# Loading the second FFN weight in chunks of 6, 5, 2 and 1 blocks of 128 rows

## Chip, cores, metric

One core of one Trainium2 chip at a time. The metric is the device time of one execution in microseconds (us). "Span" is the time from first to last instruction in a profiled execution, some 1.8 us shorter than the device time.

In the lines of the profile PE is TensorE doing matmuls, PEld its weight loads, DVE is VectorE, and SPq the queue that issues the large loads. L448 is a line of the kernel. u_ps is the result of the first FFN matmul, z_ps that of the second. A load (DMA) is cut into packets and shared out over 16 DMA engines; each of them adds 1 to the load's semaphore, a counter that other engines wait for, when its share is done. A load has landed with the 16th increment.

## The reference, cut to what matters

A decode step for 4 tokens of width 512: adaptive layer norm, attention over the last 1024 cached keys and values, then a small FFN with a gate.

```python
x = x + ga * _A_ref(h, A_k_cache, A_v_cache, A_wq, A_wo)
h = _layernorm(x, axis=-1) * (1 + cb) + sb
x = x + gb * _B_ref(h, B_w1, B_w2)      # relu(h @ w1) @ w2, w1 512x1792, w2 1792x512, bf16
```

The inputs are 32 MB, the arithmetic is small. w2's 1792 rows are 14 blocks of 128.

## The kernel before

All large loads go through one queue, in this order: keys, w_mod, wq, more keys, values, wo, w1, w2. w1 and w2 stand last; the FFN is what remains when they have landed.

```python
nc.sync.dma_start(out=w1_sb, in_=B_w1.rearrange("(p t) n -> p t n", t=DT))
E4 = 4
...
for m4 in range(FT4):                       # three chunks of 4 blocks, 512 KB each
    nc.sync.dma_start(out=w2_dst[:, m4 * E4 * D:(m4 + 1) * E4 * D], in_=w2_src[:, m4, :])
nc.sync.dma_start(...)                      # the last 2 blocks, 256 KB
...
def w1_cols(t, m):                          # a chunk of e blocks gives partition q its rows q*e .. q*e+e-1,
    f0, e = ...                             # so block m takes every e-th column of w1
    return w1_sb[:, t, f0 + m % E4:f0 + e * P:e]

def ffn1(m0, m1):     # 4 matmuls for each block, then three DVE operations for the group -> uT32
    ...
def ffn2(m0, m1):     # 4 matmuls for each block, side by side in four column groups, summed in z_ps
    ...
for (m0, m1) in [(0, 2 * E4), (2 * E4, FT)]:
    ffn1(m0, m1)
for (m0, m1) in U_GROUPS:                   # blocks 0-3, 4-7, 8-11, 12-13
    ffn2(m0, m1)
zg = z_ps * gb2 ; res = zg + x12_ps         # two DVE operations (written out in the kernel)
nc.sync.dma_start(out=out..., in_=res[::BS, :])
```

The first matmul that reads a chunk waits for the chunk's semaphore, so the chunk sizes set where PE waits.

Of the kernel before, what the change touches and what calls it, by code (L numbers as in the profile page):

```python
# [17 lines left out]
def kernel(  # L18
# [14 lines left out]
    nc = tc.nc  # L33
    P = 128
    B, Sq, D = A_x.shape
    _, Hkv, S, Dh = A_k_cache.shape
# [3 lines left out]
    Dff = B_w1.shape[1]  # L40
    DT = D // P
    FT = Dff // P
# [57 lines left out]
    for h in range(Hkv):  # L100
        vt_ = kvpool.tile([P, NI, Dh], bf16, tag="kv", name=f"v{h}")
        nc.sync.dma_start(
            out=vt_[:].rearrange("p j d -> p (j d)"),
            in_=A_v_cache[:, h, S - W:, :].rearrange("b (p j) d -> p b (j d)", j=NI),
# [13 lines left out]
    w1_sb = w12[:, 0:DT * Dff].rearrange("p (t n) -> p t n", t=DT)  # L118
    w2_sb = w12[:, DT * Dff:DT * Dff + FT * D].rearrange("p (m n) -> p m n", m=FT)
    nc.sync.dma_start(out=w1_sb, in_=B_w1.rearrange("(p t) n -> p t n", t=DT))  # L120

    E4 = 4
    FT4 = FT // E4
    F4 = FT4 * E4 * P
    w2_dst = w12[:, DT * Dff:DT * Dff + FT * D]
    w2_src = B_w2[0:F4, :].rearrange("(m q e) n -> q m (e n)", q=P, e=E4)
    for m4 in range(FT4):
        nc.sync.dma_start(out=w2_dst[:, m4 * E4 * D:(m4 + 1) * E4 * D], in_=w2_src[:, m4, :])
    nc.sync.dma_start(out=w2_dst[:, FT4 * E4 * D:FT * D], in_=B_w2[F4:Dff, :].rearrange("(q e) n -> q (e n)", q=P))
    U_GROUPS = [(m, min(m + E4, FT)) for m in range(0, FT, E4)]  # L130


    nc.scalar.preload_act_table_set("natural_log_exp_and_others")
# [87 lines left out]
    m4 = const.tile([P, B], f32, name="m4")  # L221
# [67 lines left out]
    for par in range(2):  # L289
        dst = qpad_s[:, :, par * NHW * CG:(par + 1) * NHW * CG].rearrange("p b (h c) -> p b h c", h=NHW)  # L290
        nc.vector.tensor_copy(  # L291
            out=dst[:, :, :, 16 * par:16 * par + rep],
            in_=qT_ps[:, par].rearrange("p h r b -> p b h r"))
# [35 lines left out]
    for iq in range(NQ):  # L329
        ws = slice(iq * WQ, (iq + 1) * WQ)  # L330
        nc.scalar.activation(out=e_sb[:, ws].rearrange("q (u k e) -> q u k e", k=KC, e=2),  # L331
                             in_=sc_ps[:, ws].rearrange("q (u e k) -> q u k e", e=2, k=KC), func=ACT.Exp,
# [92 lines left out]
    nc.scalar.activation(out=rstd2[:], in_=mm[:], func=ACT.Exp, scale=-0.5)  # L425

    def w1_cols(t, m):
        f0, e = (m // E4 * E4 * P, E4) if m < FT4 * E4 else (F4, 2)
        return w1_sb[:, t, f0 + m % E4:f0 + e * P:e]

    z_ps = psA.tile([NH * CG, DH2], f32, tag="t", name="z_ps")

    def ffn1(m0, m1):
        u_ps = psA.tile([P, m1 - m0, 2, B], f32, tag="t", name=f"u_ps_{m0}")
        for m in range(m0, m1):
            for t in range(DT):
                nc.tensor.matmul(out=u_ps[:, m - m0].rearrange("p s b -> p (s b)"), lhsT=w1_cols(t, m),  # L437
                                 rhs=ab[:, t].rearrange("p s b -> p (s b)"), start=(t == 0), stop=(t == DT - 1))
        us = work.tile([P, m1 - m0, B], f32, name=f"us_{m0}")
        nc.vector.tensor_tensor(out=us[:], in0=u_ps[:, :, 0, :], in1=rstd2[:].unsqueeze(1).to_broadcast([P, m1 - m0, B]),  # L440
                                op=ALU.mult)
        nc.vector.tensor_tensor(out=us[:], in0=us[:], in1=u_ps[:, :, 1, :], op=ALU.add)
        nc.vector.tensor_scalar_max(out=uT32[:, m0:m1, ::BS], in0=us[:], scalar1=0.0)

    def ffn2(m0, m1):
        for m in range(m0, m1):
            for nh in range(NH):
                nc.tensor.matmul(out=z_ps[nh * CG:(nh + 1) * CG, :], lhsT=uT32[:, m, :],  # L448
                                 rhs=w2_sb[:, m, nh * DH2:(nh + 1) * DH2],
                                 start=(m == 0), stop=(m == FT - 1), tile_position=(0, nh * CG))  # L450

    for (m0, m1) in [(0, 2 * E4), (2 * E4, FT)]:
        ffn1(m0, m1)
    for (m0, m1) in U_GROUPS:
        ffn2(m0, m1)

    zg = work.tile([NH * CG, DH2], f32, name="zg")
    nc.vector.tensor_tensor(out=zg[:], in0=z_ps[:], in1=gb2[:], op=ALU.mult)  # L458
# [33 lines left out]
```

## Time and profile before

| | before |
|---|---|
| device time, median (range) | 86.10 us (86.03 to 86.45), 3 runs; 86.19 with three more, made beside the changed kernel |
| span of the profiled run | 84.4 us |
| DMA engines busy | 90% or more from 2 to 78 us, in all slices but one |
| PE busy | 65%, off the chain of waits except at the end |

The chain and the tail's timeline are shown in the prediction. One more pair of lines: a group of the page (busy us, mean ns; then idle us ahead of it and what ended it), and the page's count of DMA packets.

```profile
L437 PE MATMUL u_ps<-ab,w 128*128 128x8 bf16 x56 | 2.0, 174 | 1.0 <-DMA w<-in_B_w_dram 1.0
DMA packets 4606, 32.14 MB, mean 381 GB/s; under 512 B 493, under 2 KB 501, under 8 KB 2037
```

### The profile page before, as it was taken

The numbers are of one execution on the slowest core, as the hardware profiler recorded it, in microseconds if no ns is written. First come the engines' busy times: TensorE is split into PE (matmuls) and PEld (weight loads), VectorE is DVE, ScalarE is ACT, GpSimd is POOL, SyncE is SP. The second block draws the span as 40 slices with busy tenths as digits, with TensorE's granted clock in tenths as the row PEclk, the third lists the DMA queues.
The fourth block names the chain that finished last, engine by engine and source line by source line (L and its number), as shares of the span: only waits on it lengthen the run. The fifth ranks groups of instructions, "written<-read, shape, count | busy, mean of one in ns | idle before, by whom it ended". The sixth has DMA issues, their size and how long they took to land.

```text
span 84.4 us, 2416 instructions
## 1 busy us (share of the span) xinstructions
PE 55.3 (65%) x1092; PEld 46.9 (56%) x1092; DVE 24.8 (29%) x70; ACT 23.1 (27%) x36; POOL 4.4 (5%) x18
## 2 busy tenths in 40 slices
PE   0029980496351899999998079994645379678640
PEld 0029970594351739788774079984542059568520
DVE  0033443013300104845546694500011020241320
ACT  2314471001200007977776376010000010020000
POOL 6940000000000000000000000000000000000000
PEclk9999999555555559999999965975555555555555
DMA  0999998999999999999999999999999999999500
GB/s 2 316 415 450 501 419 384 450 411 435 419 408 423 404 427 423 431 408 415 423 419 419 423 415 423 423 415 419 402 404 406 410 424 436 418 385 407 211 0 2
DMA packets 4606, 32.14 MB, mean 381 GB/s; under 512 B 493, under 2 KB 501, under 8 KB 2037
## 3 DMA queue, kind: packets, MB, share of 16 engines
q1 hardware_dynamic: 4580, 31.99, 91.9%
q8 instruction: 8, 0.13, 0.6%
q10 hardware_dynamic: 16, 0.01, 0.0%
q14 instruction: 2, 0.01, 0.0%
HBM read 31.99 MB, written 0.00 MB: 379 GB/s over the span
## 4 chain that ended last, share of the span: by engine, by line
DMA 92%; SPq 2%; PE 1%; DVE 1%; issue 0%
DMA v<-in_A_v_cache_dram 26%; DMA wo_sb<-in_A_wo_dram 24%; DMA wq_sb<-in_A_wq_dram 23%; DMA w<-in_B_w_dram 19%; SPq L82 1%; PE z_ps L448 1%; SPq L91 1%; DVE zg L458 0%; DVE res L460 0%
## 5 line engine op out<-in xcount | busy, mean ns | idle before, releaser
L203 ACT COPY kT<-ktp 128x1024 bf16<-128x1024 bf16 x16 | 15.5, 1017 | 15.9 <-PE ktp L198 14.9
L198 PEld LDWEIGHTS <-k 128*128 128x128 bf16 x256 | 17.3, 110 | 3.8 <-issue 2.5
L198 PE MATMUL ktp<-ident_k,k 128*128 128x128 bf16 x256 | 18.3, 241 | 1.2 <-DMA k<-in_A_k_cache_dram 1.2
L201 DVE COPY kT<-ktp 128x1024 bf16<-128x1024 bf16 x16 | 11.1, 691 | 11.9 <-PE ktp L198 11.6
L325 PE MATMUL oT_ps<-pT,v 128*128 128x16 bf16 x256 | 7.3, 172 | 2.8 <-DMA v<-in_A_v_cache_dram 1.5
L325 PEld LDWEIGHTS <-v 128*128 128x128 bf16 x256 | 7.2, 100 | 3.1 <-DMA v<-in_A_v_cache_dram 1.6
L287 PE MATMUL qT_ps<-hT,wq_sb 128*128 128x4 bf16 x128 | 3.7, 166 | 4.1 <-DMA wq_sb<-in_A_wq_dram 2.7
L287 PEld LDWEIGHTS <-wq_sb 128*128 128x128 bf16 x128 | 3.6, 104 | 4.3 <-DMA wq_sb<-in_A_wq_dram 4.3
L210 PE MATMUL sc_ps<-kT,qpad 128*32 128x512 bf16 x64 | 5.6, 445 | 0.4 <-DVE qpad L291 0.4
L342 PE MATMUL pT_ps<-ident_bf,p_rep 128*128 128x128 bf16 x32 | 3.5, 312 | 2.9 <-DVE p_rep L336 2.9
L342 PEld LDWEIGHTS <-p_rep 128*128 128x128 bf16 x32 | 3.3, 148 | 3.2 <-DVE p_rep L336 3.2
L233 PE MATMUL mT<-siluT,wmod_sb 128*128 128x4 bf16 x80 | 2.8, 173 | 3.4 <-DMA wmod_sb<-in_w_mod_dram 3.4
L233 PEld LDWEIGHTS <-wmod_sb 128*128 128x128 bf16 x80 | 2.7, 117 | 3.6 <-DMA wmod_sb<-in_w_mod_dram 3.6
L387 ACT COPY y<-y_ps 128x256 f32<-128x256 f32 x1 | 0.4, 372 | 11.9 <-DVE y L386 11.9
L382 PE MATMUL y_ps<-wo_sb,o 128*32 128x512 bf16 x16 | 2.2, 618 | 2.1 <-DMA wo_sb<-in_A_wo_dram 2.1
L173 PE MATMUL tp<-ident_bf,cx_sb 8*128 8x8 bf16 x4 | 0.3, 168 | 4.6 <-POOL qpad L162 4.6
L367 DVE TENSOR_TENSOR oT_sb<-oT_ps,rb 128x128 bf16<-128x128 f32 x1 | 0.3, 291 | 9.0 <-PE oT_ps L325 9.0
L173 PEld LDWEIGHTS <-cx_sb 8*128 8x128 bf16 x4 | 0.2, 110 | 4.6 <-issue 4.6
L336 DVE TENSOR_TENSOR p_rep<-e_sb,mi 128x512 int32<-128x512 int32 x4 | 2.5, 684 | 0.7 <-ACT e_sb L331 0.7
L437 PE MATMUL u_ps<-ab,w 128*128 128x8 bf16 x56 | 2.0, 174 | 1.0 <-DMA w<-in_B_w_dram 1.0
L448 PE MATMUL z_ps<-w,uT 128*32 128x128 bf16 x56 | 2.1, 305 | 0.7 <-DMA w<-in_B_w_dram 0.6
L390 PEld LDWEIGHTS y_ps<-sel_b,y 128*128 128x128 f32 x8 | 1.8, 327 | 1.4 <-DVE y L386 1.4
(95 smaller groups left out, 45.1 us busy)
## 6 DMA issues: line engine op xcount, KB each, us to landing
k<-in_A_k_cache_dram SPq DMA_DIRECT2D x8, 1024.0 KB, 26.1
v<-in_A_v_cache_dram SPq DMA_DIRECT2D x8, 1024.0 KB, 19.8
wq_sb<-in_A_wq_dram SPq DMA_DIRECT2D x2, 2048.0 KB, 21.6
wmod_sb<-in_w_mod_dram SPq DMA_DIRECT2D x1, 3072.0 KB, 13.7
wo_sb<-in_A_wo_dram SPq DMA_DIRECT2D x3, 1024.0 KB, 20.0
w<-in_B_w_dram SPq DMA_DIRECT2D x1, 1792.0 KB
w<-in_B_w_dram SPq DMA_DIRECT2D x3, 512.0 KB, 17.0
wo_sb<-in_A_wo_dram SPq DMA_DIRECT2D x2, 512.0 KB, 17.6
```

The source lines that it names most:

```text
L198: nc.tensor.transpose(out=tp[:, ii, :], in_=k_tiles[gi][:, iq * IQ + ii, :], identity=ident_k)
L201: nc.vector.tensor_copy(out=dst, in_=tp[:])
L203: nc.scalar.copy(out=dst, in_=tp[:])
L210: nc.tensor.matmul(out=sc_ps[hw * CG:(hw + 1) * CG, half * HALF:(half + 1) * HALF], lhsT=qpad[:, b, par, hw, :], rhs=kT[:, half * (NI // 2 ...
L233: nc.tensor.matmul(out=mT[:, k, m, :], lhsT=wmod_sb[:, t, n0:(k + 1) * D:DT], rhs=siluT32[:, t, ::BS], start=(t == 0), stop=(t == DT - 1))
L287: nc.tensor.matmul(out=qT_v[:, hq, :], lhsT=wq_sb[:, t, hq * Dh:(hq + 1) * Dh], rhs=hT[:, t, :], start=(t == 0 and hq == 0), stop=(t == DT ...
L325: nc.tensor.matmul(out=oT_ps[:, hw, par].rearrange("p b r -> p (b r)"), lhsT=v_tiles[h][:, i, :], rhs=pT[:, i, c0:c0 + B * rep], start=(fi ...
L336: nc.vector.tensor_tensor(out=p_w[:, ws, :], in0=e_w[:, ws].unsqueeze(2).to_broadcast([P, WQ // 2, B]), in1=mi4[:].unsqueeze(1).to_broadca ...
L342: nc.tensor.transpose(out=tp[:, ii, :], in_=p_rep[:, i // 2, :, i % 2], identity=ident_bf[:])
L382: nc.tensor.matmul(out=y4_ps[l * CG:(l + 1) * CG, :], lhsT=o4[:, l, h % NHW, h // NHW, :], rhs=wo_sb[:, h, l, :], start=(h == 0), stop=(h ...
L437: nc.tensor.matmul(out=u_ps[:, m - m0].rearrange("p s b -> p (s b)"), lhsT=w1_cols(t, m), rhs=ab[:, t].rearrange("p s b -> p (s b)"), star ...
L448: nc.tensor.matmul(out=z_ps[nh * CG:(nh + 1) * CG, :], lhsT=uT32[:, m, :], rhs=w2_sb[:, m, nh * DH2:(nh + 1) * DH2], start=(m == 0), stop= ...
```

## The change

The intent: what stands behind the last landing cannot be hidden, so let the last chunk be as small as possible, and let the chunks ahead of it shrink towards it so that PE has caught up when it lands. The number of loads stays.

```diff
-    E4 = 4
...
-    for m4 in range(FT4):
-        nc.sync.dma_start(out=w2_dst[:, m4 * E4 * D:(m4 + 1) * E4 * D], in_=w2_src[:, m4, :])
-    nc.sync.dma_start(out=w2_dst[:, FT4 * E4 * D:FT * D], ...)
+    W2_CHUNKS = [(0, 6), (6, 5), (11, 2), (13, 1)]
+    for (m0, e) in W2_CHUNKS:
+        nc.sync.dma_start(out=w2_dst[:, m0 * D:(m0 + e) * D],
+                          in_=B_w2[m0 * P:(m0 + e) * P, :].rearrange("(q e) n -> q (e n)", e=e))
...
-        return w1_sb[:, t, f0 + m % E4:f0 + e * P:e]
+        m0, e = [ch for ch in W2_CHUNKS if ch[0] <= m][-1]
+        return w1_sb[:, t, m0 * P + m - m0:(m0 + e) * P:e]
...
-    for (m0, m1) in [(0, 2 * E4), (2 * E4, FT)]:
+    for (m0, m1) in [(0, 6), (6, FT)]:
         ffn1(m0, m1)
-    for (m0, m1) in U_GROUPS:
-        ffn2(m0, m1)
+    for (m0, e) in W2_CHUNKS:
+        ffn2(m0, m0 + e)
```

More of the change, by code (lines that the diff above doesn't have):

```diff
@@ L120 @@
     nc.sync.dma_start(out=w1_sb, in_=B_w1.rearrange("(p t) n -> p t n", t=DT))
-    E4 = 4
-    FT4 = FT // E4
-    F4 = FT4 * E4 * P
+    W2_CHUNKS = [(0, 6), (6, 5), (11, 2), (13, 1)]
+    assert sum(e for _, e in W2_CHUNKS) == FT
     w2_dst = w12[:, DT * Dff:DT * Dff + FT * D]
-    w2_src = B_w2[0:F4, :].rearrange("(m q e) n -> q m (e n)", q=P, e=E4)
-    for m4 in range(FT4):
-        nc.sync.dma_start(out=w2_dst[:, m4 * E4 * D:(m4 + 1) * E4 * D], in_=w2_src[:, m4, :])
-    nc.sync.dma_start(out=w2_dst[:, FT4 * E4 * D:FT * D], in_=B_w2[F4:Dff, :].rearrange("(q e) n -> q (e n)", q=P))
-    U_GROUPS = [(m, min(m + E4, FT)) for m in range(0, FT, E4)]
+    for (m0, e) in W2_CHUNKS:
+        nc.sync.dma_start(out=w2_dst[:, m0 * D:(m0 + e) * D],
+                          in_=B_w2[m0 * P:(m0 + e) * P, :].rearrange("(q e) n -> q (e n)", e=e))
     nc.scalar.preload_act_table_set("natural_log_exp_and_others")
@@ L427, in w1_cols @@
     def w1_cols(t, m):
-        f0, e = (m // E4 * E4 * P, E4) if m < FT4 * E4 else (F4, 2)
-        return w1_sb[:, t, f0 + m % E4:f0 + e * P:e]
+        m0, e = [ch for ch in W2_CHUNKS if ch[0] <= m][-1]
+        return w1_sb[:, t, m0 * P + m - m0:(m0 + e) * P:e]
     z_ps = psA.tile([NH * CG, DH2], f32, tag="t", name="z_ps")
```

## The prediction

> **What bounds the kernel now.** I read the page's slices first, then the chain that ended last, then the queue's own waits, then the tail in the timeline. The slices say what kind of kernel this is:
>
> ```profile
> DMA  0999998999999999999999999999999999999500
> GB/s 2 316 415 450 501 419 384 450 411 435 419 408 423 404 427 423 431 408 415 423 419 419 423 415 423 423 415 419 402 404 406 410 424 436 418 385 407 211 0 2
> ```
>
> A slice is 84.4 / 40 = 2.11 us. The 16 DMA engines are full from the second slice to the 37th and half full in the 38th (78.1 to 80.2 us), at about 420 GB/s. The chain agrees: 92% of it is DMA, and of the compute only what follows the last loads is on it.
>
> ```profile
> 64.38 15.68 DMA w<-in_B_w_dram
> 80.06 0.04 issue
> 80.10 0.62 PE z_ps L448 x16
> 80.72 0.02 issue
> 80.74 0.43 PE z_ps L448 x8
> 81.17 0.02 issue
> 81.19 0.30 DVE zg L458
> 81.49 0.02 issue
> 81.52 0.29 DVE res L460
> ```
>
> Columns: start, length, what. The third w2 chunk (blocks 8 to 11) lands at 80.06 and releases 16 matmuls, 4 per block; then come the 8 matmuls of the last chunk (blocks 12, 13), then two DVE operations, and the output store. The chain puts the last 8 matmuls down to the 16 before them. That needs a second look, because matmul ends are modelled and matmuls overlap. The timeline of the tail:
>
> ```profile
> 80.37 0.15 PEld L448 LDWEIGHTS <-uT 128*32 128x32 bf16 x1
> 80.74 0.14 PEld L448 LDWEIGHTS <-uT 128*32 128x32 bf16 x7 [0.22 <-issue]
> 81.19 0.29 DVE L458 TENSOR_TENSOR zg<-z_ps,gb 128x128 f32<-128x128 f32 x1 [2.19 <-PE z_ps L448]
> ```
>
> The weight loads, which are not modelled that way, stop at 80.52 and stand idle 0.22 us until 80.74. The last of the 16 matmuls was issued at 80.404, the first of the 8 only at 80.738. So what the 8 waited for is the last chunk itself. The trace's semaphore records give its landing: 80.69. The same records give w1 76.28, and w2's four chunks 77.57, 78.85, 80.06, 80.69. That sequence, at the pace of the slowest DMA engine (1.29, 1.28, 1.21 us for 512 KB; 0.63 for 256 KB), sets the end: last landing 80.69, 0.05 to the first matmul, 0.41 for two blocks (80.738 to 81.143), 0.05 to DVE, then a fixed rest.
>
> The work before it has room. The other end of the tail:
>
> ```profile
> 76.33 1.98 PE L437 MATMUL u_ps<-ab,w 128*128 128x8 bf16 x56 [0.97 <-DMA w<-in_B_w_dram]
> 78.41 1.10 PE L448 MATMUL z_ps<-w,uT 128*32 128x128 bf16 x32
> 80.10 1.04 PE L448 MATMUL z_ps<-w,uT 128*32 128x128 bf16 x24 [0.59 <-DMA w<-in_B_w_dram]
> ```
>
> The first FFN matmul starts as w1 lands; the second FFN matmul has done blocks 0 to 7 by 79.51 and idles 0.59 us for data.
>
> **What the Trainium skill says.** "DMA: Bandwidth & Descriptors", section "Why a DMA increments its semaphore by 16 and not by 1", says that the 16 engines finish independently and only the full count means landed. The trace agrees strongly: the last chunk's 16 increments come from 78.74 to 80.69, so the slowest engine is 1.95 us behind the fastest. Therefore I use times of the 16th increment only. "Perfetto Trace Analysis", section "DMA Optimizations", says two things that pull apart here: transfers under 2 KB have significant overhead, and splitting can let some work start sooner. For the first, this trace has 2 KB packets in the tail at 84 ns (median) against 162 for 4 KB, and 1 KB packets only in the loads of c and x, at 46: a small loss per byte, no cliff. "TensorE: Matmul & The Clock Gate", section "Weight-path perf modes — Fast Weight Load (FWL) and DoubleRow", says the fast weight load reads packed or strided chunks, and gives no cost for the stride. The trace shows one: first-FFN matmuls follow each other at 33 ns where w1 columns are 4 apart (8 bytes) and at 27 ns where they are 2 apart.
>
> **The change, part by part.**
>
> 1. *Number of things.* The loads stay four, all queued on the same sequencer far ahead. The same 56 + 56 matmuls, and three DVE operations in each of two groups, stand in the same order. Moved are only the points where the second FFN matmul waits for a chunk (blocks 6, 11, 13 in place of 4, 8, 12) and the group border of the first FFN matmul (6 in place of 8). Comparing the instruction order of both builds confirms this.
>
> 2. *Bytes and packets.* w2 is 1792 KB either way and has 8 packets per engine and chunk either way: 3 x 4 KB + 2 KB before, 6 + 5 + 2 + 1 KB after. From 4 KB (162 ns) and 8 KB (312 ns) the cost is 36.6 ns per KB above a constant; by that line I estimate 237 ns for 6 KB and 200 for 5 KB, and take 84 and 46 as measured. Eight sets: 8 x (237 + 200 + 84 + 46) = 4.54 us against 8 x (3 x 162 + 84) = 4.56. So the last landing moves by -0.02 us, to about 80.67.
>
> 3. *Landings in between*, estimated with the measured pace of 0.315 us per 128 KB block from w1's 76.28: chunk 0 at 78.17, chunk 1 at 79.74, chunk 2 at 80.36, chunk 3 at 80.67.
>
> 4. *First FFN matmul.* If spacing stays 33 ns it ends at 78.31 as now. The first group, 24 matmuls, ends near 77.3, its DVE chain (0.69 us before) near 78.05. The second group's chain (0.18 + 0.18 + 0.22 with gaps, 0.65) ends near 79.0. Chunk 0 lands at 78.17, so the second FFN matmul starts at about 78.4 as now, and blocks 0 to 5 take 0.1 us each, to 79.1. No saving here, because PE then waits for chunk 1 at 79.74.
>
> 5. *After the last landings.* A block of four matmuls takes 107 ns (80.158, 80.264, 80.371 are starts of successive blocks). Blocks 6 to 10 start at 79.79 and are issued by 80.3. Blocks 11 and 12 wait for 80.36, start at 80.41 and are issued by 80.6. Block 13 waits for 80.67 and starts at 80.72. Before, two blocks followed the last landing, 0.41 us; now one, 0.41 - 0.107 = 0.30. So the last matmul ends at 81.02 in place of 81.14: -0.11 for the block, -0.02 for the landing.
>
> 6. *The rest*: zg, res and the store are as before.
>
> The sum: 86.10 - 0.13 = 85.97 us, a gain of 0.15%.
>
> **The rivals.**
>
> *The chain is read literally*: the 16 matmuls after chunk 2 were the bound, and shrinking chunk 2 from 4 to 2 blocks gives two more blocks, 0.21 us, to about 85.8 in all. Against it: the 0.22 us gap in weight loads, and the issue times. PE cannot end before the last landing whatever its order.
>
> *Small packets at the end cost more than the line says.* One c/x packet of 1 KB took 154 ns, and two 2 KB packets in the tail took 228 and 231. If all eight 1 KB packets took 84 rather than 46, the last landing comes 0.3 us later, and the change is a loss of 0.2: 86.3. Against it: nothing in the tail shows such a floor, and eight engines are already idle then.
>
> *A wider stride in w1 reads.* Columns are now 6 and 5 apart (12 and 10 bytes) for 44 of 56 matmuls. If 33 ns became 45, the first FFN matmul ends 0.5 us later, near 78.8; the second group's DVE chain ends at 79.5, still ahead of chunk 1's 79.74. It would be hidden. Only beyond some 55 ns does it pass that landing, and then blocks 6 to 10 still have 0.3 us of room before chunk 2. So 86.0 again.
>
> *Instruction fetch.* The trace has 16 KB instruction packets of 1.0 to 1.1 us on single DMA engines, and after each one more engine lags by over a microsecond. The last comes at 78.39. If one fell on an already late engine in the tail, the end would go to about 87. The instruction count is unchanged, so I see no reason for it to fall differently.
>
> **The range and the chances.** The three runs before span 86.03 to 86.45, more than the predicted gain. I centre on 86.0 and take 85.7 (the literal chain plus favourable packets) to 86.35 (the small-packet loss). Two per cent is 1.72 us. The whole path from last landing to the second DVE operation is 1.12 us, so faster by 2% would need less DMA time, and no bytes go: 0.005. Slower by 2% would need a tail engine delayed twice: 0.01. Within: 0.985.
>
> **What would show it right or wrong.** In the changed kernel's tail: last landing within 0.1 us of 4.4 us after w1's; 4 matmuls after it, ending about 0.30 us after they start; a visible gap in weight loads ahead of them; PE idle ahead of block 6. A last landing over 4.6 us after w1's would mean that the small packets cost; PE running without a gap from block 6 to block 13 would mean the compute side became the bound; over 1 us of extra lag would mean the instruction fetch.

## The result, and the profile after

The changed kernel took 86.06 us in the median of 6 runs (86.00 to 86.20), the kernel before 86.19 in the 6 runs it is compared with. The ratio is 0.9987, 95% interval 0.9968 to 1.0006. Repeated with 5 rounds, see `after_again` below: 86.06 against 86.09, ratio 0.9991, 0.9977 to 1.0004. Both point the same way, and both intervals contain 1: the gain is not shown by the times. (An estimate from both, each weighted by the width of its interval, is 0.9990, 0.9979 to 1.0001.) It has to be read in the tail of the trace.

The timeline of PE alone, changed kernel, answers to the three PE lines in the prediction:

```profile
76.16 2.41 PE L434 MATMUL u_ps<-ab,w 128*128 128x8 bf16 x56 [0.93 <-DMA w<-in_B_w_dram]
78.49 0.83 PE L445 MATMUL z_ps<-w,uT 128*32 128x128 bf16 x24
79.59 1.32 PE L445 MATMUL z_ps<-w,uT 128*32 128x128 bf16 x32 [0.28 <-DMA w<-in_B_w_dram]
```

The idle time is now ahead of block 6 (after 24 matmuls), as the new chunk border says. The first FFN matmul is longer, 2.41 us in place of 1.98. The end of the timeline, from 80.5 us on:

```profile
80.62 0.11 PEld L445 LDWEIGHTS <-uT 128*32 128x32 bf16 x3
80.97 0.29 DVE L455 TENSOR_TENSOR zg<-z_ps,gb 128x128 f32<-128x128 f32 x1 [1.68 <-PE z_ps L445]
81.29 0.29 DVE L457 TENSOR_TENSOR res<-zg,x_ps 128x128 bf16<-128x128 f32 x1
```

The weight loads at 80.62 are those of block 13 alone. From them to the first DVE operation 0.35 us pass; before, from 80.74 to 81.19, it was 0.45. The gap in the weight loads ahead of block 13, which the prediction named as a sign, is there but only 0.13 us long (80.50 to 80.62 in the instruction times), too short for the longer timelines to set it apart.

The chain of waits after is worth a look because it misleads:

```profile
79.55 0.04 issue
79.59 1.35 PE z_ps L445 x31
80.94 0.02 issue
80.97 0.30 DVE zg L455
81.27 0.02 issue
81.29 0.29 DVE res L457
```

It says that chunk 1, landing at 79.55, released 1.35 us of PE work without a break. The issue times in the same trace say otherwise: first matmul of each block at 79.595, 79.657, 79.764, 79.870, 79.977 (blocks 6 to 10), 80.285, 80.345 (11, 12), 80.621 (13). Blocks follow each other at 107 ns, with two jumps of about 0.3 us, each 0.04 us after a landing (80.24 and 80.58). Each matmul is drawn 0.3 us long and they overlap, so their ends cover the gaps, and the chain does not see a wait where two drawn matmuls touch. With pipelined matmuls, starts tell more than ends.

A table of the tail, from the semaphore records (a landing is the 16th increment) and instruction times, in us; it will serve for the experiments too:

| kernel | w1 lands | last of w2 lands | between | last matmul's end after that | second DVE operation to end of span | w1's landing to end of span |
|---|---|---|---|---|---|---|
| before | 76.28 | 80.69 | 4.42 | 0.45 | 2.61 | 8.13 |
| changed | 76.11 | 80.58 | 4.47 | 0.34 | 2.60 | 8.08 |
| after_again | 76.23 | 80.67 | 4.44 | 0.34 | 2.60 | 8.04 |
| e1_last_first | 76.25 | 80.67 | 4.42 | 1.82 | 2.61 | 9.51 |
| e2_split_last | 76.10 | 80.65 | 4.55 | 0.34 | 2.76 | 8.31 |
| e2_again | 76.32 | 80.80 | 4.48 | 0.34 | 2.76 | 8.24 |
| e9_split_last_wo4 | 76.34 | 80.78 | 4.44 | 0.34 | 2.61 | 8.05 |
| e3_w1_contig | 76.18 | 80.60 | 4.42 | 0.34 | 2.61 | 8.03 |
| e4_stride14 | 76.19 | 80.56 | 4.37 | 1.02 | 2.60 | 8.66 |
| e5_1kb | 76.43 | 81.41 | 4.98 | 0.34 | 2.61 | 8.59 |
| e6_few_engines | 76.06 | 80.99 | 4.92 | 0.34 | 2.78 | 8.71 |
| e7_three_chunks | 76.30 | 80.69 | 4.39 | 0.67 | 2.67 | 8.39 |
| e8_one_op | 76.33 | 80.73 | 4.40 | 0.34 | 2.60 | 7.68 |

Differences are taken before rounding, so some stand 0.01 us off those of the rounded times (as the 4.41 and 2.77 us that the expectations quote). The two DVE operations between the fifth and sixth columns take 0.66 us in all of them but the last, which has one. w1's landing differs by 0.37 us among kernels that do the same until then. That is noise of the load phase, and it is larger than the gain looked for. Of the 0.22 us by which the changed kernel's span is shorter, 0.17 are that noise; counted from w1's landing, the gain is 0.05 us, 0.09 in the repetition.

### The profile page after: what moved, and what is told of

Read it like the earlier page. It is cut to its first block, busy times and chain, and to the rows that moved or that the text cites. A ratio compares the mean times of both kernels' runs of the same rounds, so it can differ in the third digit from the quotient of the medians.

```text
span 84.2 us, 2416 instructions
## 1 busy us (share of the span) xinstructions
PE 55.5 (66%) x1092; PEld 46.9 (56%) x1092; DVE 24.7 (29%) x70; ACT 23.2 (28%) x36; POOL 4.4 (5%) x18
## 4 chain that ended last, share of the span: by engine, by line
DMA 73%; PE 19%; SPq 3%; DVE 1%; issue 1%; DVEq 0%
DMA wq_sb<-in_A_wq_dram 28%; DMA v<-in_A_v_cache_dram 24%; DMA w<-in_B_w_dram 21%; PE ktp L195 11%; PE sc_ps L207 4%; PE qT_ps L284 2%; PE z_ps L445 2%; SPq L82 1%; SPq L91 1%; SPq L95 1%; DVE zg L455 0%; DVE res L457 0%; DVE qpad L288 0%; DVEq L288 0%
## 5 line engine op out<-in xcount | busy, mean ns | idle before, releaser
L339 PEld LDWEIGHTS <-p_rep 128*128 128x128 bf16 x32 | 2.5, 123 | 3.5 <-DVE p_rep L333 3.4
L434 PEld LDWEIGHTS <-w 128*128 128x128 bf16 x56 | 2.3, 131 | 1.1 <-DMA w<-in_B_w_dram 1.1
```

Source lines behind the costliest of these rows:

```text
L339: nc.tensor.transpose(out=tp[:, ii, :], in_=p_rep[:, i // 2, :, i % 2], identity=ident_bf[:])
L434: nc.tensor.matmul(out=u_ps[:, m - m0].rearrange("p s b -> p (s b)"), lhsT=w1_cols(t, m), rhs=ab[:, t].rearrange("p s b -> p (s b)"), star ...
```

## The experiments

Theory A: the end is the last landing, plus a fixed 0.34 us for one block, plus 0.107 us for each further block that had to wait for it; the rest of the FFN is hidden behind landings. Rivals: PE was the bound, as the chain says; the growth of the first FFN matmul eats part of the gain; small packets cost more than they save.

### e1_last_first: all blocks behind the last landing

```diff
-    for (m0, e) in W2_CHUNKS:
+    for (m0, e) in [(13, 1), (0, 6), (6, 5), (11, 2)]:
         ffn2(m0, m0 + e)
```

The accumulation's first and last block move along (13 and 12).

> The changed kernel, but the second FFN matmul takes block 13, whose data land last, first; so all 14 blocks stand behind the last landing in place of one. Theory (the end is the last landing plus 0.30 us for the first block and 0.107 us for each further one): 13 x 0.107 = 1.39 us more, about 87.45 us, a ratio of 1.015 to the kernel before; in the trace the last matmul ends about 1.7 us after the last landing (0.34 in the changed kernel). Rival (the matmuls overlap so well that their number behind the landing hardly matters, and the gain of the change is noise): under 0.3 us more. Rival (the chain read literally, PE as the bound before the last landing): no later than the sum of what was idle, so also well under 1 us.

Right result, 87.48 us, ratio 1.0147 (1.0132 to 1.0163). PE's timeline:

```profile
76.30 2.40 PE L434 MATMUL u_ps<-ab,w 128*128 128x8 bf16 x56 [0.96 <-DMA w<-in_B_w_dram]
80.81 1.68 PE L445 MATMUL z_ps<-w,uT 128*32 128x128 bf16 x56 [2.11 <-DMA w<-in_B_w_dram]
```

PE idles 2.11 us, then does all 56 matmuls after the landing at 80.67. Blocks start 107 ns apart, and the last ends 1.82 us after the landing, against 0.34: 1.48 us for 13 blocks. 1.39 were expected from the block interval; the rest is that the first matmul started 0.14 us after the landing here, and 0.04 in the changed kernel. So the price of a block behind the last landing is shown on a scale well above the noise.

### e3_w1_contig: the first FFN matmul made short (wrong result)

```diff
-        return w1_sb[:, t, m0 * P + m - m0:(m0 + e) * P:e]
+        return w1_sb[:, t, m * P:(m + 1) * P]
```

> The changed kernel with w1's columns read one beside the other (2 bytes apart) for every block; a wrong result on purpose, as hidden units then meet the wrong rows of w2. The first FFN matmul took 2.41 us in the changed kernel (47 ns from matmul to matmul at 12 bytes, 40 at 10, 27 at 4 and 2) against 1.98 before. Theory (it is hidden behind the landings of w2): 27 ns throughout, about 1.6 us in all, and the same time within 0.1 us, about 86.05. Rival (the 0.43 us that it grew by ate a part of the gain): 0.1 to 0.4 us faster than the changed kernel, about 85.7 to 85.9.

86.10 us, ratio 0.9987 (0.9969 to 1.0006), the same as the changed kernel. Everything that the program records of this line (duration min, median, max in ns), kernel before first, then the changed kernel, then this one:

```profile
L437 PE MATMUL u_ps<-ab,w x56: 167/174/195, 76.3 to 78.1; 128*128 128x8 bf16 x56
```
```profile
L434 PE MATMUL u_ps<-ab,w x56: 167/181/209, 76.2 to 78.4; 128*128 128x8 bf16 x56
```
```profile
L434 PE MATMUL u_ps<-ab,w x56: 167/168/189, 76.2 to 77.7; 128*128 128x8 bf16 x56
```

The starts of the first and last one, 76.3 to 78.1, 76.2 to 78.4 and 76.2 to 77.7, show the length, the durations hardly do: the cost of a stride is in the interval between matmuls. 0.75 us less work here (2.41 to 1.66) moved nothing. So the growth of the first FFN matmul in the changed kernel is hidden, and the rival falls.

### e4_stride14: where the hiding ends

```diff
-  in_=B_w2[m0 * P:(m0 + e) * P, :].rearrange("(q e) n -> q (e n)", e=e))
+  in_=B_w2.rearrange("(q m) n -> q (m n)", m=FT)[:, m0 * D:(m0 + e) * D])
...
-        return w1_sb[:, t, m0 * P + m - m0:(m0 + e) * P:e]
+        return w1_sb[:, t, m::FT]
```

> The changed kernel with the same four chunks and packets, but partition q of w2 holds rows 14q to 14q+13, so that w1's columns are read 14 apart (28 bytes); a right result. Theory (the interval grows by about 3.4 ns for each byte above 8): some 100 ns from matmul to matmul, 5.7 us for the first FFN matmul, which then ends near 81.9 and is no longer hidden: about 2.6 us more, 88.7. Rival (the cost of the stride stops growing at 16 bytes or so): 60 ns, 3.4 us, ends near 79.6, second group ready at 80.3, blocks 6 to 13 end about 81.4: 0.5 us more, 86.5. Second rival (always hidden): 86.05.

Right result, 86.72 us, ratio 1.0058 (1.0041 to 1.0075). My theory of 100 ns fell: the interval is 60 ns, as the first rival said. Over all kernels, the interval between these matmuls is 27 ns at 2 and 4 bytes, 33 at 8, 40 at 10, 47 at 12, 53 at 14 (in e7_three_chunks) and 60 at 28. From 8 to 14 bytes it grows about 3.3 ns a byte, from 14 to 28 by 7 ns in all; where between them the growth ends was not measured.

```profile
79.79 0.19 DVE L436 TENSOR_TENSOR us<-u_ps,rstd 128x32 f32<-128x32 f32 x1 [1.19 <-PE u_ps L433]
80.24 0.24 DVE L439 TENSOR_SCALAR uT<-us 128x32 bf16<-128x32 f32 x1
80.53 0.78 PEld L444 LDWEIGHTS <-uT 128*32 128x32 bf16 x32 [0.29 <-DVE uT L439]
```

In this stretch of the timeline PE waits no longer for data but for the second group's DVE chain, which ends at 80.48: 8 blocks follow that, and the matmuls end 1.02 us after the last landing. So the slack of the first FFN matmul is limited: 0.43 us of growth were free, 1.54 were not.

### e2_split_last: the last chunk alone split

Chunks 4, 4, 4, 1, 1 in place of 4, 4, 4, 2, with the first FFN's groups of 8 and 6 as before. (Edits here are against the changed kernel.)

```diff
-    W2_CHUNKS = [(0, 6), (6, 5), (11, 2), (13, 1)]
+    W2_CHUNKS = [(0, 4), (4, 4), (8, 4), (12, 1), (13, 1)]
...
-    for (m0, m1) in [(0, 6), (6, FT)]:
+    for (m0, m1) in [(0, 8), (8, FT)]:
```

> The kernel before with only its last chunk of 2 blocks split into 1 and 1 (chunks 4, 4, 4, 1, 1; strides of 8 bytes for 12 blocks, 2 bytes for 2; first FFN groups of 8 and 6 as before). Theory: the end of the matmuls is 0.30 us after the first matmul behind the last landing, as in the changed kernel, so the same gain of about 0.1 us (86.0 to 86.1, not to be told from the kernel before by its time), with the first FFN matmul back at 2.0 us. It also tells whether the last landing, 4.47 us after that of w1 in the changed kernel against 4.41 before, comes later because of 1 KB packets: two chunks of them here, so about 4.5 us if they cost, 4.4 if that was chance. Rival (the large early chunks are what pays): no gain in the trace, matmuls end 0.4 us after the last landing.

86.27 us, ratio 1.0005 (0.9989 to 1.0021). The matmuls end 0.34 us after the last landing, as in the changed kernel: that saving comes with the small last chunk alone. Yet the kernel was not faster. The table shows two terms going the other way: 4.55 us between the landings, and 2.76 us from the second DVE operation to the end, in place of 2.61. The latter was not in my theory. The instruction times explain it: when the store is issued, the queue waits for the eight semaphores of the loads in six waits, one after the other, each about 0.06 us when nothing is left to wait for. The semaphores are handed out in turn. With 4 chunks the store has the one that is waited for last; with 5 it has one in the third wait, and three waits follow it. Two runs tested this.

> The split of the last chunk alone (4, 4, 4, 1, 1), once more. In its first trace the last matmul ended 0.34 us after the last landing as expected, but the last landing came 4.55 us after w1's (4.41 before), and from the second DVE operation to the end of the span 2.77 us passed (2.61 before): the store had another semaphore, and the queue's final waits, one after the other, met it in the third place and not in the last, with three more waits of 0.06 us after it. Theory: both recur; landing 4.5 to 4.55 us after w1's, 2.77 us after the last DVE operation, and the same time as the kernel before or 0.1 us more. Rival (chance): landing 4.42, 2.61, and 0.1 us under the kernel before.

86.38 us, ratio 1.0023 (1.0010 to 1.0037): slower than the kernel before by 0.2 us, where 0 to 0.1 was expected; here the interval leaves out 1, in the first run it did not. 4.48 us between landings, 2.76 us at the end.

> The same five chunks of w2 (4, 4, 4, 1, 1), with the first two loads of wo made one, so that the number of loads is that of the kernel before and the store gets the semaphore that the queue waits for last. Theory (the place of the store's semaphore costs 0.17 us): 2.61 us from the second DVE operation to the end of the span, 0.17 us under the run beside it, 86.05 to 86.1. Rival (the 2.77 us belong to the five chunks themselves): 2.77 us and the same time as the run beside it. The landing after w1's should be as in the run beside it, 4.5 to 4.55 us, if two chunks of 1 KB packets cost 0.1 us.

```diff
-    WO_CHUNKS = [(0, 2), (2, 4), (4, 6), (6, 7), (7, 8)]
+    WO_CHUNKS = [(0, 4), (4, 6), (6, 7), (7, 8)]
```

86.25 us, ratio 1.0008 (0.9995 to 1.0021), 0.13 us under the run beside it; 2.61 us at the end. The 86.05 to 86.1 us that were expected were missed: it is not shown to be faster than the kernel before. Yet from w1's landing on its trace takes 8.05 us, as the changed kernel's do (8.08 and 8.04). So in the trace the small last chunk with an unchanged number of loads gives the whole gain, without graded chunks ahead of it. Why the times do not follow stays open; w1 landed late in this trace, at 76.34, and the changed loads of wo were not tested by themselves. The queue's own waits (us in all, times, longest), kernel before first, then e2_again:

```profile
SPq L487 <- DMA out_dram<-res: 0.7, 1, 0.7
```
```profile
SPq L484 <- DMA out_dram<-res: 0.9, 1, 0.9
```

The wait for the store looks longer by 0.2 us in the second because it begins earlier, at 82.696, with the other semaphores still to come. So the place of the store's semaphore is worth 0.16 us, more than the 0.107 that the split saves. The changed kernel avoids it by keeping four chunks. The landing distance (4.55, 4.48, 4.44 with two chunks of 1 KB packets; a mean of 4.42 over six traces with the packets of the changed kernel) overlaps with the spread of those six, 4.37 to 4.47: a cost of 0.07 us is possible, not shown.

### e5_1kb: every packet of w2 1 KB

```diff
-  out=w2_dst[:, m0 * D:(m0 + e) * D], in_=B_w2[...].rearrange("(q e) n -> q (e n)", e=e)
+  out=w2_sb[:, m0:m0 + e, :],         in_=B_w2[...].rearrange("(e q) n -> q e n", e=e)
...
+        return w1_sb[:, t, m * P:(m + 1) * P]
```

> The changed kernel with the same four chunks, but partition q of a block holds its row q, so that every packet of w2 is 1 KB (14 x 8 per engine in place of 4 x 8 of 6, 5, 2 and 1 KB) and w1's columns are read one beside the other; a right result. Theory (46 ns for a packet of 1 KB, as for the few in the changed kernel): 112 x 46 = 5.15 us against 4.54, so the last landing comes about 5.1 us after that of w1 in place of 4.47, 0.6 us more in all, about 86.65. Rival (small packets have a cliff, 84 ns or more each): 9.4 us, over 4 us more, about 90. Rival (packets overlap and their number costs nothing): 86.05.

Right result, 86.75 us, ratio 1.0059 (1.0042 to 1.0076). The page's packet counts of the changed kernel, then of this one:

```profile
DMA packets 4605, 32.14 MB, mean 382 GB/s; under 512 B 492, under 2 KB 628, under 8 KB 2036
```
```profile
DMA packets 5885, 32.14 MB, mean 378 GB/s; under 512 B 492, under 2 KB 2292, under 8 KB 3316
```

1280 packets more, 80 for each engine, and the last landing comes 0.56 us later after w1's (4.98 against the mean of 4.42): 7 ns for each further packet. The median packet of 1 KB took 49 ns. There is no cliff. The 8 small packets per engine in the changed kernel take the place of 8 others, so they cost nothing that can be seen. The five chunks of e2 and e9 are 40 packets per engine in place of 32; by the 7 ns an estimate for them is 0.06 us, which would account for the 0.07 us left open there.

### e6_few_engines: who is the slowest engine

```diff
+    for (q0, q1) in [(0, 119), (119, 128)]:     # in place of the last chunk's one load
+        nc.sync.dma_start(out=w2_dst[q0:q1, 13 * D:14 * D], in_=B_w2[13 * P + q0:13 * P + q1, :])
```

> The changed kernel with the last block of w2 loaded by two DMAs, of 119 partitions and of 9. The engines are divided by the largest number up to 16 that divides the outer size, so 7 engines should carry 17 packets of 1 KB each, 17 x 46 = 0.78 us, and 9 engines one packet each. In the changed kernel 7 engines had landed chunk 2 by 78.6, the others only from 78.95 to 80.24. Theory (the slowest engine sets the end, whoever it is): if the 7 are among the early ones, the last landing is about 80.3 in place of 80.58 and the time 0.3 us shorter, 85.75; if a late one is among them, about 81.0 to 81.1, 0.45 us longer, 86.5. Which of the two is not known before; the increments of this DMA's semaphore tell it. Rival (the spread between engines is an artefact of the records): the last landing moves by less than 0.1 us in either direction.

86.69 us, ratio 1.0057 (1.0040 to 1.0074): the second case. The larger DMA's semaphore got 7 increments from engines, which is what the rule in the Trainium skill, "DMA: Bandwidth & Descriptors", section "Why a DMA increments its semaphore by 16 and not by 1", gives for 119 partitions (the largest number up to 16 that divides them); they came at 79.30, 79.46, 79.46, 79.51 and 80.51, 80.78, 80.79. Four engines were early and three late, in one small transfer. The load of 9 partitions, queued behind it, was the last to land, at 80.99. The timeline of weight loads shows the price:

```profile
80.56 0.14 PEld L447 LDWEIGHTS <-uT 128*32 128x32 bf16 x7 [0.21 <-issue]
81.03 0.11 PEld L447 LDWEIGHTS <-uT 128*32 128x32 bf16 x4 [0.33 <-DMA w<-in_B_w_dram]
```

The last block waits until 81.03. A landing that is 0.45 us later (4.92 against 4.47) and 0.17 from the store's semaphore (five loads again) make up the 0.63 us by which the median is above the changed kernel's. The rival's forecast, under 0.1 us, fell. But this does not by itself show that the spread is real: 9 further packets of 46 ns would be 0.41 us for equal engines too. What speaks for the spread are the increments, and, without semaphores, the packet records of the kernel before: its DMA engines are busy 93% from 77.5 to 78.75 us and 46% from 78.75 to 80.0. It cannot be used in this way, since late engines are among the ones that a smaller division keeps.

### e7_three_chunks: the small last chunk without the small ones ahead of it

```diff
-    W2_CHUNKS = [(0, 6), (6, 5), (11, 2), (13, 1)]
+    W2_CHUNKS = [(0, 7), (7, 6), (13, 1)]
...
-    for (m0, m1) in [(0, 6), (6, FT)]:
+    for (m0, m1) in [(0, 7), (7, FT)]:
```

> The changed kernel with w2 in three chunks of 7, 6 and 1 blocks (first FFN groups of 7 and 7; strides of 14, 12 and 2 bytes). The last landing is followed by one block as in the changed kernel, but the 6 blocks before it may only start with chunk 1, which lands 0.31 to 0.34 us before the last. Theory (all of it is queued on PE): matmuls end 0.04 + 0.30 + 6 x 0.107 = 0.98 us after chunk 1's landing, that is 0.65 us after the last landing in place of 0.34; with 8 packets per engine fewer the last landing may come 0.1 us sooner; so 0.2 to 0.3 us more than the changed kernel, about 86.3, and no gap in PE between chunk 1's blocks and the last. Rival (only the size of the last chunk counts): 86.05 or 0.1 less.

86.48 us, ratio 1.0042 (1.0029 to 1.0056). PE's timeline of the last 28 matmuls:

```profile
80.43 0.94 PE L445 MATMUL z_ps<-w,uT 128*32 128x128 bf16 x28 [0.33 <-DMA w<-in_B_w_dram]
```

Here PE really is the bound: blocks start at 107 ns from 80.489 on without a jump, block 13 at 81.02 although its data landed at 80.69, and the end is 0.67 us after the landing (0.65 expected). That is why the changed kernel has a chunk of 2 between 5 and 1. The median is 0.42 us above the changed kernel's, and the trace explains 0.33 from w1's landing on: 0.33 on PE and 0.07 at the end, less 0.07 for an earlier landing. The 0.07 at the end are the store's semaphore again: with three chunks it is in the last wait but one (2.67 us). The rest is within the spread of w1's landing.

### after_again: the changed kernel once more

> The changed kernel once more, to narrow its interval. Theory (one block of 0.107 us less behind the last landing, which comes 4.4 us after w1's as before): 0.1 us under the kernel before, a ratio of 0.9988. If the ratio is 1.000 or more, the gain in the trace is given back somewhere.

86.06 us, ratio 0.9991 (0.9977 to 1.0004). The ratio came as expected, the interval still contains 1.

### e8_one_op: one operation less behind the last landing

If all that stands behind the last landing counts one to one, the two DVE operations there are the next thing to shorten.

```diff
+    nc.vector.scalar_tensor_tensor(out=rgb[:], in0=gb2[:], scalar=0.0, in1=gb2[:], op0=ALU.is_equal, op1=ALU.add)
+    nc.vector.reciprocal(out=rgb[:], in_=rgb[:])            # early, right after gb2
...
+    nc.vector.tensor_tensor(out=xg[:], in0=x12_ps[:], in1=rgb[:], op=ALU.mult)
+    nc.tensor.matmul(out=z_ps[:], lhsT=ident_f[:], rhs=xg[:], start=True, stop=False)   # before ffn1
...
-                                 start=(m == 0), stop=(m == FT - 1), tile_position=(0, nh * CG))
+                                 start=False, stop=(m == FT - 1), tile_position=(0, nh * CG))   # in ffn2
...
-    nc.vector.tensor_tensor(out=zg[:], in0=z_ps[:], in1=gb2[:], op=ALU.mult)
-    nc.vector.tensor_tensor(out=res[:], in0=zg[:], in1=x12_ps[:], op=ALU.add)
+    nc.vector.tensor_tensor(out=res[:], in0=z_ps[:], in1=gb2[:], op=ALU.mult)
```

> The changed kernel with one DVE operation less behind the last matmul: x divided by the gate is added into the accumulation by a matmul with the identity while PE waits for w1, so that one product with the gate ends the kernel (reciprocal of the gate made early; rows with a gate of zero kept finite). A right result. Theory (all behind the last landing counts one to one): 0.32 us less (0.29 for the operation and 0.03 to the next), about 85.75, a ratio of 0.995. Rival (the added matmul[...], some 0.5 us by the kernel's other fp32 matmuls, delays the first FFN matmul beyond its slack, or the reciprocal delays the query path): 86.05 or more.

Right result (a gate of exactly zero in a used row would lose x there; none occurs in these inputs, as the result shows). 85.75 us, ratio 0.9964 (0.9951 to 0.9977), 0.31 us under the changed kernel run beside it in the median (0.23 by the two ratios). Its timeline:

```profile
75.82 0.80 PE L454 MATMUL z_ps<-xg,ident_f 128*128 128x128 f32 x2 [0.38 <-DVE xg L432]
76.41 2.39 PE L439 MATMUL u_ps<-ab,w 128*128 128x8 bf16 x56
79.81 1.26 PE L450 MATMUL z_ps<-w,uT 128*32 128x128 bf16 x32 [0.25 <-DMA w<-in_B_w_dram]
81.12 0.29 DVE L461 TENSOR_TENSOR res<-z_ps,gb 128x128 bf16<-128x128 f32 x1 [1.60 <-PE z_ps L450]
```

The added matmul fills time in which PE waited for w1, and PE still waits 0.25 us for chunk 1. One DVE operation ends the kernel. It beats both kernels, and unlike the change itself the times show it: the interval leaves out 1.

## Why the prediction was right

- *The last chunk's landing, and not PE, sets the end.* Right. e1 and the block starts after show it; the chain read literally was the rival that fell, and e7 shows what a trace looks like where it would hold.
- *One block less behind the last landing, 0.11 us.* Right: first matmul to last end was 0.41 us before (80.738 to 81.143), 0.30 after (80.621 to 80.920), and e1 shows 107 ns between blocks on a large scale.
- *Last landing earlier by 0.02 us.* The trace had it 0.05 later from w1's landing (4.47 against 4.42). Over six traces with these packets the mean is 4.42, from 4.37 to 4.47, against a single trace of the kernel before. Nothing moved that can be seen; the term was too small to be predicted, and harmless. e5 confirms the way of reckoning: by packets, with a small constant for each. Two slips in the working did no harm: the slope from 162 and 312 ns is 37.5 ns per KB and not 36.6 (the 237 and 200 were worked out with 37.5; the changed kernel's trace has medians of 236 and 200), and the sum of 4.56 us is 0.14 above the 4.42 measured, but only the difference of two such sums was used.
- *First FFN matmul.* The text took 33 ns "if spacing stays" and named a stride rival at 45. The rival came true (47 and 40 ns, end at 78.56), and with it the conclusion that it would be hidden: e3. e4 shows that the slack is finite. There my extrapolation of the interval was wrong: 60 ns, not 100. The limit of "some 55 ns" does not follow from the prediction's own numbers either: from 79.0 to 79.74 over 44 matmuls are 17 ns, so 50; and the room left after it, 80.3 to 80.36, was 0.06 us and not 0.3.
- *The sum, -0.13 us.* Measured in medians -0.13 and -0.03 in two comparisons, by the ratios 0.11 and 0.08 us, none clear of zero; in the trace, counted from w1's landing, 0.05 and 0.09. The direction and order of size agree, the exact size stays open. That the first comparison hit -0.13 was luck: in that pair of traces 0.17 us came from w1's landing, which the change does not touch. The stated range holds the kernel before too, so the time alone does not test the mechanism; the trace and e1 do.
- *What the prediction did not see*: that keeping the number of loads at four matters. I noted that the number stays, and did not know that a fifth load costs 0.16 us at the end through the place of the store's semaphore (e2, e9).
- *Instruction fetch.* The last fetch came at 78.39 again and the spread of the last chunk's landings was as before (78.72 to 80.58). That fetches make engines late is not tested here; it is only that one more engine lags after each. It is worth a test: the last engine lands 1.95 us after the first in the kernel before, and one block is 0.107.

## What to carry to other kernels

In a kernel that is bound by loads to its end, count only what must wait for the last landing, and make that small: the last chunk, and every operation after it; and see that the compute has caught up by then (e7 shows a case where it has not). A gain so found is at most the work removed from behind that point, here 0.1% of the time, so look first at how many microseconds stand there at all. Check afterwards that a changed number of loads has not moved something else, such as the order of the final waits.

## What the Trainium skill lacked or had wrong

- "TensorE: Matmul & The Clock Gate", section "Weight-path perf modes — Fast Weight Load (FWL) and DoubleRow", allows packed or strided weights and gives no price for the stride; the page "SBUF — State Buffer" speaks of a penalty for strided accesses, but gives none in ns for weight loads. Here, with 128 columns of bf16 and 8 columns of moving data at a granted clock of 0.5, the interval was 27 ns at 2 and 4 bytes, 33 at 8, 40 at 10, 47 at 12, 53 at 14, 60 at 28.
- "Perfetto Trace Analysis", section "DMA Optimizations", speaks of significant overhead for transfers under 2 KB and gives no size for it; for packets of larger transfers "DMA: Bandwidth & Descriptors" has a per-packet overhead, worked out for 256 B. Here, in a full queue, 1 KB packets throughout w2 (1792 KB) cost 0.56 us, 7 ns for each further packet. No transfer under 128 KB was tried.
- No page that I read has the engines' spread that builds up in a long load phase: the last chunk's increments came from 78.74 to 80.69 in the kernel before. The packets of the instruction queues go with it: eight of 16 KB, 1.0 to 1.1 us each, and one of 8 KB, 0.34 us, start between 19.55 and 78.39 us, and the number of engines that land over 0.9 us after the first grows from 0 to 9 over the loads, by one after each of them. The cause was not tested. ("Runtime: NRT & Kernel Launch", section "Instruction fetch mechanics", has the fetch in 16 KB blocks, but nothing of what it does to loads.)
- No page that I read has the final waits of the issuing queue: 0.05 to 0.07 us for each wait that comes after the store's, 0.16 us for the three here.
